# Wide products in the output phase of a recurrent-memory transformer kernel, and left output sums moved to an earlier phase

## The chip, the cores and the metric

The kernel runs on one core of a Trainium2 chip. The metric is the time of one execution in device microseconds. Engines named below: TensorE (PE; its weight loads are PEld), VectorE (DVE), ScalarE (ACT), GpSimd (POOL) and SyncE (SP). SP issues the large transfers, POOL the small ones, ACT those of some intermediate results.

## The reference

The input `x` has 2048 rows of 1024 values. It is normalized by rows (`xn`). Three parts are added: `x` itself, a recurrent attention part A, and a part B that adds a routed feed-forward result to two rows.

Part A is what fills the time. The rows are cut into 64 segments of 32 rows, and 8 rows of memory stand before each:

```python
for s in range(n_seg):
    h = jnp.concatenate([mem, xs], axis=1)          # 8 + 32 rows
    q, k, v = h @ Wq, h @ Wk, h @ Wv                # 32 heads of 128
    p = softmax(mask(q @ k.T * scale))
    o = (p @ v) @ Wo
    mem = o[:, :M, :]                               # the next segment's memory
    outs.append(o[:, M:, :])
```

The memory of one segment is the output of the one before, so the 64 segments follow each other strictly. The four weight matrices are 8 MB each in bf16. Part B picks two rows by a router, and runs them through a gated feed-forward layer at the end.

## The kernel before

**Granules.** The weights are cut into 64 granules of 128 x 2048 values (512 KB): 0 to 47 for q, k and v in the six phases q0, k0, q1, k1, v0, v1 of eight granules each (`PHASES`), and 48 to 63 for the output matrix, two heads each. 44 granules stay in SBUF (`wres`). The 20 of `STREAMED` are read again in every segment from a DRAM copy (`wsc`) into five slots (`g`, `fetch`, L366). A slot's next transfer is issued by SP when PE has released the slot. Granule 6 and half of granule 25 are kept in PSUM instead and copied back by ScalarE and VectorE (`bring_back`, L389; `kept_piece`, L393).

**A segment.** For each granule of a phase four products of 512 columns (L817) add into one PSUM bank, one for each group of 32 columns of the array. PSUM tiles of the tag `acc` have two buffers, used in turn. At the end of a phase ScalarE copies the bank out (XB at L836, VM at L846); PE transposes it (L649), and copies make QT and KT. Scores (L672, L674) and softmax run beside the later phases, `attend` (L736 to L747) beside v1 and the output phase. In the output phase each granule w = 0 to 15 has eight products (`project`, L586): two heads, each 256 columns for each of the four column groups, so that row group g of the bank holds output columns 256 g to 256 g + 255. Then VectorE adds the bank to X, which holds the residual (L885). The result OB is stored by POOL (L887), and its memory rows are transposed (L301) and copied into ST (L324), the left operand of the next segment. Only then can the next segment begin.

**Left rows.** A segment's 32 rows of input are split: 24 go with the 8 rows of memory through the products above. The q, k and v of the other 8 rows don't depend on the memory. Those of four segments (a group, j = 0 to 3) are gathered into 32 rows ahead of time, and their attention outputs likewise behind the group; both take their products through the weights in *passes*: one more set of four products for a granule (`left_pass`, L579, for q, k, v; `project_left`, L598, for the output). The table `PASSES` names for each unit (q0, ..., o) the place (j, phase, granule in the phase) of each pass; phases 7 and 8 stand for the end of a segment, before and after the memory is transposed. These passes fill PE there while VectorE makes L885 and the copy to ST. `COPIES` names the place and the engine that takes a finished unit out of PSUM (`copy_unit`, L627). For q and k units the copy XBl is then stored to DRAM by ACT (`ql_d<-XBl`, L628); a copy by VectorE has its store put off until ScalarE has made VM. The output unit is finished in the first segment of the next group: in `sum_left` the residual OL is prepared by VectorE (L347), two ScalarE copies (L616), two VectorE adds (L619) and one GpSimd add (L620) bring the two halves together, and POOL stores them.

**Order.** The order of every engine's work is that of the program text; `hook(p, kc, fn)` puts `fn` behind granule kc of phase p. Tiles of the pool `one` have one buffer for each tag, and a new tile of a tag waits until all accesses of the last one have ended, transfers included. Three tags (`bx`, `vl0`, `vl1`) change roles from group to group (`roles`); `roles[0]` holds BK, BX or XL, and XBl in turn.

Of the kernel before, what the change touches and what calls it, by code (L numbers as in the profile page):

```python
# [9 lines left out]
F32 = mybir.dt.float32  # L10
# [7 lines left out]
N_RES = 44  # L18
N_SLOT = 5
KEPT_WHOLE = 6  # L20
KEPT_PART = 25
# [22 lines left out]
}  # L44

COPIES = {"q0": (1, 1, 0, "scalar"), "q1": (1, 5, 7, "vector"), "k0": (2, 2, 0, "scalar"), "k1": (2, 5, 7, "vector"),
          "v0": (3, 4, 7, "scalar"), "v1": (3, 5, 7, "scalar"), "o": (0, 3, 3, "vector")}


@with_exitstack  # L50
def kernel(
# [17 lines left out]
    P = 128  # L69
# [203 lines left out]
    def two_rows(m, tag):  # L273
# [3 lines left out]
        return t  # L277

    def load_seg(s):
        for g in range(4):  # L280
            nc.gpsimd.dma_start(out=X[s % 2][32 * g:32 * g + XM, :],  # L281
                                in_=x2[s * SEG:s * SEG + XM, 256 * g:256 * (g + 1)])

# [42 lines left out]
    def load_left(G, t, crossed=False):  # L326

        o4 = x2[4 * G * SEG:4 * (G + 1) * SEG, :].rearrange("(s r) d -> s r d", s=4)[:, XM:SEG, :]
        if not crossed:
            o4 = o4.rearrange("s r d -> r s d")  # L330
        for g in range(4):
            b = 2 * (g % 2) + g // 2 if crossed else g
            nc.gpsimd.dma_start(out=t[32 * g:32 * (g + 1), :], in_=o4[:, :, 256 * b:256 * (b + 1)])
        return t
# [103 lines left out]
    for g in range(4):  # L438
        nc.gpsimd.dma_start(out=OB[32 * g + XM:32 * g + SEG, :], in_=A_mem0[0, :, 256 * g:256 * (g + 1)])
    n_x = 1  # L440
# [140 lines left out]

    def project(PS, w, Gv, lhs, last, first=False):
        for hs in range(2):
            h = 2 * w + hs
            for g in range(4):
                nc.tensor.matmul(PS[32 * g:32 * g + 32, 0:256], lhsT=lhs(h),  # L586
                                 rhs=Gv[:, D * hs + 256 * g:D * hs + 256 * (g + 1)], start=(first and hs == 0),
                                 stop=(last and hs == 1), tile_position=(0, 32 * g), skip_group_check=True)

# [11 lines left out]
    def copy_unit(u, s, engine):  # L601
# [10 lines left out]
        elif u == "o":  # L612
            OL = xl_of[0]
            LF = one.tile([P, 256], F32, tag="otl", name="LF")
            for c in range(2):
                nc.scalar.copy(out=LF[64 * c:64 * c + 64, :], in_=PS[64 - 64 * c:128 - 64 * c, 256 * c:256 * c + 256])  # L616
            for c in range(2):
                here = slice(64 * c, 64 * c + 64)
                nc.vector.tensor_tensor(out=LF[here, :], in0=PS[here, 256 * c:256 * c + 256], in1=LF[here, :], op=ALU.add)  # L619
            nc.gpsimd.tensor_tensor(out=OL[:, :], in0=LF[:, :], in1=OL[:, :], op=ALU.add)  # L620
            o4 = out2[4 * Gu * SEG:4 * (Gu + 1) * SEG, :].rearrange("(s r) d -> s r d", s=4)
            for g in range(4):
                b = 2 * (g % 2) + g // 2
                nc.gpsimd.dma_start(out=o4[:, XM:SEG, 256 * b:256 * (b + 1)], in_=OL[32 * g:32 * (g + 1), :])
# [7 lines left out]
    for s in range(NSEG):  # L632
# [176 lines left out]
        for p, (mat, half) in enumerate(PHASES):  # L809
# [3 lines left out]
            for kc in range(KC):  # L813
                g = 8 * p + kc
                Gv = back if s > 0 and g == KEPT_WHOLE else granule(g)
                for jq in range(4):
                    nc.tensor.matmul(PSm[32 * jq:32 * jq + 32, :], lhsT=ST[:, kc, :], rhs=part(Gv, jq),  # L817
                                     start=(kc == 0), stop=(kc == KC - 1), tile_position=(0, 32 * jq))
# [45 lines left out]
        for w in range(16):  # L864
# [19 lines left out]
        OB = X[s % 2]  # L884
        nc.vector.tensor_tensor(out=OB[:, :], in0=WO[:, 0:256], in1=OB[:, :], op=ALU.add)  # L885
        for g in range(4):
            nc.gpsimd.dma_start(out=out2[s * SEG:s * SEG + XM, 256 * g:256 * (g + 1)], in_=OB[32 * g:32 * g + XM, :])  # L887
        run_passes(7, 0)
# [125 lines left out]
```

## Time and profile before

| | |
|---|---|
| median of 3 runs | 1865.73 us (1863.98 to 1869.82) |
| profiled execution | 1871.21 us, span 1869.1 us |
| mean granted clock | 0.957 |
| PE, PEld busy | 84%, 45% |
| DVE, ACT, POOL busy | 48%, 37%, 24% |
| DMA | 712.27 MB, mean 381 GB/s |

Times are from the span's start. A row of the timeline has start, length, engine, line, operation, what is written and read, the shape and the number of instructions; in brackets is the idle time of the engine before, and what ended it. A row of a table of stretches has the stretch, its length, the busy time of PE, PEld, DVE, ACT and POOL with the number of instructions, the granted clock, the DMA share and GB/s. A row of waits has who waited for whom, the total, the number and the longest.

### The profile page before, as it was taken

To read this page: it belongs to the slowest core of one execution; us is meant where nothing else is said; L and a number is where in the kernel's file an instruction comes from. 1 tells how busy PE (TensorE), PEld (TensorE's weight loads), DVE (VectorE), ACT (ScalarE), POOL (GpSimd) and SP (SyncE) were. 2 spreads that over 40 slices of the span, in tenths; PEclk is the share of its full clock that TensorE was granted. 3 is DMA by queue.
4 is the path that set the end of the run, shared out by engine and by line. 5 is a ranking of instruction groups with operands and counts; after the bars stand their busy time and mean duration, and the time that the engine had idled before them with its cause. 6 is when DMAs were issued, how large, how long until landed. Compare 5 with 4: busy or idle time off the path is not lost.

```text
span 1869.1 us, 80529 instructions
## 1 busy us (share of the span) xinstructions
PE 1568.8 (84%) x34978; PEld 847.9 (45%) x34978; DVE 896.9 (48%) x2950; ACT 683.6 (37%) x1933; POOL 457.1 (24%) x898
## 2 busy tenths in 40 slices
PE   3458998898998988888899988988889988988764
PEld 1124444444444444444444444444445544444433
DVE  6725544554455444544554455544544455445430
ACT  1113433444343433434344334434334343433320
POOL 3111322213231322223132322323132221312220
PEclk8669999999999999999999999999999999999995
DMA  9999999999999999999999999999999999999998
GB/s 370 406 355 373 388 386 380 393 382 387 394 385 392 366 383 391 359 380 385 388 375 388 389 384 387 373 396 374 378 369 396 394 382 383 378 377 352 384 402 338
DMA packets 230322, 712.27 MB, mean 381 GB/s; under 512 B 39040, under 2 KB 52912, under 8 KB 229968
## 3 DMA queue, kind: packets, MB, share of 16 engines
q1 hardware_dynamic: 192592, 671.18, 93.0%
q0 software_dynamic: 28736, 28.08, 4.7%
q10 hardware_dynamic: 8640, 7.87, 1.2%
q8 instruction: 274, 4.49, 0.9%
q14 instruction: 80, 0.66, 0.1%
HBM read 694.32 MB, written 22.29 MB: 383 GB/s over the span
## 4 chain that ended last, share of the span: by engine, by line
DMA 61%; PE 32%; DVE 4%; issue 1%; ACT 1%; SPq 0%; ACTq 0%; DVEq 0%
DMA g<-wsc 54%; PE PSm L817 17%; PE WO L586 4%; PE PSl L579 4%; PE BT L649 2%; DMA XP<-in_A_x_dram 2%; PE WL L598 1%; DMA MW<-in_B_w_gate_dram 1%; DVE XR L256 1%; DMA MW<-in_B_w_up_dram 1%; DMA g<-in_A_Wq_dram 1%; DMA wres<-in_A_Wo_dram 1%; DMA g<-in_A_Wo_dram 1%; DMA MW<-in_B_w_down_dram 1%; DMA g<-in_B_w_down_dram 1%
## 5 line engine op out<-in xcount | busy, mean ns | idle before, releaser
L817 PE MATMUL PSm<-wres,ST 128*32 128x512 bf16 x8448 | 700.5, 383 | 6.5 <-DMA wres<-in_A_Wv_dram 3.5
L817 PEld LDWEIGHTS <-ST 128*32 128x32 bf16 x12288 | 323.6, 96 | 412.7 <-issue 168.2
L817 PE MATMUL PSm<-g,ST 128*32 128x512 bf16 x3588 | 360.0, 386 | 97.7 <-DMA g<-wsc 76.3
L586 PEld LDWEIGHTS <-OT 128*32 128x32 bf16 x8192 | 217.6, 97 | 166.6 <-issue 141.0
L836 ACT CAST XB<-PSm 128x512 bf16<-128x512 f32 x256 | 150.7, 589 | 283.9 <-PE PSm L817 280.8
L586 PE MATMUL WO<-wres,OT 128*32 128x256 bf16 x5632 | 237.6, 278 | 12.3 <-DMA wres<-in_A_Wo_dram 8.0
L495 POOL DMA_DIRECT2D LX<-ql_d x63 | 35.4, 562 | 814.0 <-PE WO L586 423.2
L586 PE MATMUL WO<-g,OT 128*32 128x256 bf16 x2560 | 133.3, 281 | 84.1 <-DMA g<-wsc 72.6
L579 PE MATMUL PSl<-wres,STL 128*32 128x512 bf16 x2112 | 184.5, 390 | 0.4 <-issue 0.4
L887 POOL DMA_DIRECT2D out_dram<-X x256 | 130.2, 515 | 211.9 <-DVE X L885 169.4
L664 DVE COPY KT<-BT 128x512 bf16<-128x512 bf16 x112 | 45.9, 410 | 278.7 <-issue 121.8
L281 POOL DMA_DIRECT2D X<-in_A_x_dram x256 | 130.1, 515 | 179.6 <-PE PSm L817 88.8
L389 ACT COPY BK<-KEPT 128x512 bf16<-128x512 bf16 x126 | 74.3, 590 | 131.2 <-PE WO L586 99.8
L657 ACT COPY QT<-BT 128x512 bf16<-128x512 bf16 x128 | 75.0, 586 | 127.1 <-PE BT L502 78.1
L649 PEld LDWEIGHTS <-XB 128*128 128x128 bf16 x1024 | 58.6, 98 | 117.1 <-ACT XB L836 75.2
L885 DVE TENSOR_TENSOR X<-WO,X 128x256 bf16<-128x256 f32 x64 | 27.2, 425 | 172.3 <-PE WO L586 172.3
L649 PE MATMUL BT<-IDENT,XB 128*128 128x128 bf16 x1024 | 102.2, 223 | 8.2 <-ACT XB L836 6.7
L579 PEld LDWEIGHTS <-STL 128*32 128x32 bf16 x3072 | 84.0, 98 | 53.0 <-issue 8.5
L846 ACT CAST VM<-PSm 128x512 bf16<-128x512 f32 x128 | 76.5, 598 | 83.3 <-PE PSm L817 82.8
L736 PEld LDWEIGHTS <-VM 32*128 32x128 bf16 x2048 | 65.1, 91 | 83.7 <-issue 72.7
L393 DVE COPY g<-KEPT 128x512 bf16<-128x512 bf16 x126 | 47.6, 420 | 101.7 <-PE PSm L817 51.5
L681 DVE TENSOR_TENSOR BS<-BS,CT 128x96 f32<-128x96 f32 (+1 forms) x256 | 59.1, 231 | 72.8 <-PE BS L674 68.3
(175 smaller groups left out, 2371.9 us busy)
## 6 DMA issues: line engine op xcount, KB each, us to landing
g<-wsc SPq DMA_DIRECT2D x1134, 512.0 KB, 6.0
g<-wsc SPq DMA_DIRECT2D x63, 256.0 KB, 5.7
LX<-ql_d POOLq DMA_DIRECT2D x63, 128.0 KB, 5.6
ql_d<-XBl ACTq DMA_DIRECT2D x60, 128.0 KB, 5.8
MW<-in_B_w_gate_dram SPq DMA_DIRECT2D x16, 448.0 KB, 9.5
MW<-in_B_w_up_dram SPq DMA_DIRECT2D x16, 448.0 KB, 9.1
wres<-in_A_Wk_dram SPq DMA_DIRECT2D x12, 512.0 KB, 11.9
MW<-in_B_w_down_dram SPq DMA_DIRECT2D x12, 512.0 KB, 10.1
```

The costliest lines, as they stand in the source:

```text
L281: nc.gpsimd.dma_start(out=X[s % 2][32 * g:32 * g + XM, :], in_=x2[s * SEG:s * SEG + XM, 256 * g:256 * (g + 1)])
L389: copy(out=back[c][:, :], in_=KEPT_COLS[KEPT_WHOLE][c])
L579: nc.tensor.matmul(PSl[32 * jq:32 * jq + 32, :], lhsT=STL[:, g % KC, :], rhs=part(Gv, jq), start=first_, stop=last_, tile_position=(0, 32 ...
L586: nc.tensor.matmul(PS[32 * g:32 * g + 32, 0:256], lhsT=lhs(h), rhs=Gv[:, D * hs + 256 * g:D * hs + 256 * (g + 1)], start=(first and hs == ...
L649: nc.tensor.transpose(out=PTq[:, il, :, :].rearrange("p j r -> p (j r)"), in_=XB[:, il * P:(il + 1) * P], identity=IDENT[:, :])
L657: nc.scalar.copy(out=QT[half][:, :, :], in_=pv)
L681: nc.vector.tensor_tensor(out=S4, in0=S4, in1=m, op=ALU.add)
L736: nc.tensor.matmul(o, lhsT=VM[half][q0:q0 + 32, il * P:(il + 1) * P], rhs=PTm[q0:q0 + 32, il, 0:NK], start=True, stop=False, tile_position ...
L817: nc.tensor.matmul(PSm[32 * jq:32 * jq + 32, :], lhsT=ST[:, kc, :], rhs=part(Gv, jq), start=(kc == 0), stop=(kc == KC - 1), tile_position= ...
L836: nc.scalar.copy(out=XB[:, :], in_=PSm[:, :])
L846: nc.scalar.copy(out=VM[half][:, :], in_=PSm[:, :])
L887: nc.gpsimd.dma_start(out=out2[s * SEG:s * SEG + XM, 256 * g:256 * (g + 1)], in_=OB[32 * g:32 * g + XM, :])
```

## The change

For the first twelve granules of the output phase `project` makes four products of 512 columns in place of eight of 256: the even head goes to row groups 0 and 1, the odd head to 2 and 3, each with both halves of the columns. The two heads' halves then have to be added across partitions (`add_halves`, four VectorE adds of 64 x 256 each): the first two take the bank's halves crosswise and add X, the other two add the straight halves. The result is an f32 tile SUM with the tag `roles[0]`. The last four granules keep the eight products, in a second PSUM tile, and the last add takes SUM in place of X. Since the halves fall into another order, blocks 1 and 2 of 256 columns change places (`block`) in X, in the memory and in the output's stores.

The output unit's last six passes and its copy move ahead in the first segment of a group: the last pass from phase 3 to phase 1, the copy to the end of phase 1, `sum_left` to its middle. The kept pieces of granule 25 are copied one phase earlier. `copy_unit` for the output unit uses `add_halves`: two ScalarE copies, two VectorE adds and the GpSimd add become four VectorE adds. The q0 passes of segment 0's end are made there, no longer in segment 1.

```diff
-          (3, 8, 0): [52, 54], (0, 0, 7): [55], (0, 1, 3): [57], (0, 1, 7): [58], (0, 2, 3): [60], (0, 2, 6): [61],
-          (0, 3, 2): [63]},
+          (3, 8, 0): [52, 54], (0, 0, 3): [55], (0, 0, 7): [57], (0, 1, 2): [58], (0, 1, 4): [60], (0, 1, 5): [61],
+          (0, 1, 6): [63]},
-          "v0": (3, 4, 7, "scalar"), "v1": (3, 5, 7, "scalar"), "o": (0, 3, 3, "vector")}
+          "v0": (3, 4, 7, "scalar"), "v1": (3, 5, 7, "scalar"), "o": (0, 1, 7, "vector")}
+    def block(g):
+        return 2 * (g % 2) + g // 2
-                if s == 0:
+                if s == 0 and at[0] < 7:
                     after_first.append((u, g))
+    def project(PS, w, Gv, lhs):
         for hs in range(2):
             h = 2 * w + hs
+            if w < N_WIDE:
+                for c in range(2):
+                    r0 = 64 * hs + 32 * c
+                    nc.tensor.matmul(PS[r0:r0 + 32, :], lhsT=lhs(h), rhs=Gv[:, D * hs + 512 * c:D * hs + 512 * (c + 1)],
+                                     start=(w == 0), stop=(w == N_WIDE - 1), tile_position=(0, r0), skip_group_check=True)
+                continue
             for g in range(4):
...
+    def add_halves(PS, src, mid, dst):
+        for out, a, flip in ((mid, src, True), (dst, mid, False)):
+            for c in range(2):
+                here = slice(64 * c, 64 * c + 64)
+                there = slice(64 - 64 * c, 128 - 64 * c) if flip else here
+                nc.vector.tensor_tensor(out=out[here, :], in0=PS[there, 256 * c:256 * c + 256], in1=a[here, :], op=ALU.add)
...
-            for c in range(2):
-                nc.scalar.copy(out=LF[64 * c:64 * c + 64, :], in_=PS[64 - 64 * c:128 - 64 * c, 256 * c:256 * c + 256])
-            for c in range(2):
-                here = slice(64 * c, 64 * c + 64)
-                nc.vector.tensor_tensor(out=LF[here, :], in0=PS[here, 256 * c:256 * c + 256], in1=LF[here, :], op=ALU.add)
-            nc.gpsimd.tensor_tensor(out=OL[:, :], in0=LF[:, :], in1=OL[:, :], op=ALU.add)
+            add_halves(PS, OL, LF, OL)
...
-            hook(2, 3, lambda: sum_left(xl_of[0], G - 1))
+            hook(1, 3, lambda: sum_left(xl_of[0], G - 1))
...
-            hook(2, 1, lambda: kept_piece(KEPT_PART, 2, nc.vector.tensor_copy))
-            hook(2, 2, lambda: kept_piece(KEPT_PART, 3, nc.vector.tensor_copy))
+            hook(1, 1, lambda: kept_piece(KEPT_PART, 2, nc.vector.tensor_copy))
+            hook(1, 2, lambda: kept_piece(KEPT_PART, 3, nc.vector.tensor_copy))
...
-            project(WO, w, Gv, lhs_main, w == 15, first=(w == 0))
+            if w == N_WIDE:
+                SUM = one.tile([P, 256], F32, tag=roles[0], name="SUM")
+                add_halves(WO, X[s % 2], SUM, SUM)
+                WO = psA.tile([P, 512], F32, tag="acc", name="WO")
+            project(WO, w, Gv, lhs_main)
...
-        nc.vector.tensor_tensor(out=OB[:, :], in0=WO[:, 0:256], in1=OB[:, :], op=ALU.add)
+        nc.vector.tensor_tensor(out=OB[:, :], in0=WO[:, 0:256], in1=SUM[:, :], op=ALU.add)
```

More of the change, by code (lines that the diff above doesn't have):

```diff
@@ L19 @@
 N_SLOT = 5
+N_WIDE = 12
 KEPT_WHOLE = 6
@@ L331, in load_left @@
         for g in range(4):
-            b = 2 * (g % 2) + g // 2 if crossed else g
+            b = block(g) if crossed else g
             nc.gpsimd.dma_start(out=t[32 * g:32 * (g + 1), :], in_=o4[:, :, 256 * b:256 * (b + 1)])
@@ L438 @@
     for g in range(4):
-        nc.gpsimd.dma_start(out=OB[32 * g + XM:32 * g + SEG, :], in_=A_mem0[0, :, 256 * g:256 * (g + 1)])
+        nc.gpsimd.dma_start(out=OB[32 * g + XM:32 * g + SEG, :], in_=A_mem0[0, :, 256 * block(g):256 * (block(g) + 1)])
     n_x = 1
@@ L816 @@
                 for jq in range(4):
-                    nc.tensor.matmul(PSm[32 * jq:32 * jq + 32, :], lhsT=ST[:, kc, :], rhs=part(Gv, jq),
+                    nc.tensor.matmul(PSm[32 * jq:32 * jq + 32, :], lhsT=ST[:, 2 * block(kc // 2) + kc % 2, :], rhs=part(Gv, jq),
                                      start=(kc == 0), stop=(kc == KC - 1), tile_position=(0, 32 * jq))
@@ L884 @@
         OB = X[s % 2]
-        nc.vector.tensor_tensor(out=OB[:, :], in0=WO[:, 0:256], in1=OB[:, :], op=ALU.add)
+        nc.vector.tensor_tensor(out=OB[:, :], in0=WO[:, 0:256], in1=SUM[:, :], op=ALU.add)
         for g in range(4):
-            nc.gpsimd.dma_start(out=out2[s * SEG:s * SEG + XM, 256 * g:256 * (g + 1)], in_=OB[32 * g:32 * g + XM, :])
+            nc.gpsimd.dma_start(out=out2[s * SEG:s * SEG + XM, 256 * block(g):256 * (block(g) + 1)], in_=OB[32 * g:32 * g + XM, :])
         run_passes(7, 0)
```

10 lines of the change are left out of this document (5 added, 5 removed).

## The prediction

> **What bounds the kernel now.** I read the page first (share by engine, transfers, chain), then the table of stretches for two segments, then the order of time around one segment's end. A segment is one pass of the loop over 32 rows; there are 64.
>
> ```profile
> span 1869.1 us, 80529 instructions
> PE 1568.8 (84%) x34978; PEld 847.9 (45%) x34978; DVE 896.9 (48%) x2950; ACT 683.6 (37%) x1933; POOL 457.1 (24%) x898
> DMA  9999999999999999999999999999999999999998
> q8 instruction: 274, 4.49, 0.9%
> DMA 61%; PE 32%; DVE 4%; issue 1%; ACT 1%; SPq 0%; ACTq 0%; DVEq 0%
> PE BT L301 <- DVE X L885: 2.1, 4, 0.5
> PE PSm L817 <- DMA g<-wsc: 76.3, 154, 2.5
> PE WO L586 <- DMA g<-wsc: 72.6, 150, 2.0
> ```
>
> The DMA engines are 90% busy or more in nearly every slice, and the chain that ended last is 61% DMA. TensorE stands for streamed weights 149 us in all (the last two rows). So weight transfers set most of the pace. VectorE and ScalarE are half idle. But the pace differs by stage:
>
> ```profile
> 1011.04:1016.36 5.32, 4.99 (x88) 2.44 (x88) 1.02 (x3) 1.66 (x3) 1.79 (x5) 1.00 1.02 395
> 1016.36:1021.71 5.35, 5.22 (x117) 2.47 (x113) 2.14 (x6) 2.87 (x6) 2.01 (x4) 1.00 0.94 319
> 1028.52:1036.24 7.72, 5.33 (x170) 4.03 (x170) 3.50 (x15) 2.22 (x9) 0.55 (x1) 1.00 1.02 409
> PE WO L586 <- DMA g<-wsc: 2.4, 3, 1.3
> ```
>
> This is segment 34 (the third of a group of four): the first two phases, the next two, and the output phase. After the length stands PE's busy time; the last number is GB/s. In the first and third stretch data move at 395 and 409 GB/s and PE stands still 0.33 and 2.39 us. In the second PE is busy 5.22 of 5.35 us and the rate is only 319: there the five slots of streamed weights come free at PE's pace. PE time taken out of the output phase is therefore worth nothing by itself; a delay of PE ahead of the second stretch can pass through.
>
> **The wide products.** Twelve of sixteen output granules go from 8 products of 256 columns to 4 of 512. TensorE, at the end of segment 33 and the start of 34:
>
> ```profile
> 1007.73 0.40 PE L586 MATMUL WO<-g,OT 128*32 128x256 bf16 x8 [0.44 <-DMA g<-wsc]
> 1007.95 0.62 PE L586 MATMUL WO<-wres,OT 128*32 128x256 bf16 x16
> 1009.18 0.40 PE L586 MATMUL WO<-g,OT 128*32 128x256 bf16 x8 [0.61 <-DMA g<-wsc]
> 1009.40 0.40 PE L586 MATMUL WO<-wres,OT 128*32 128x256 bf16 x8
> 1009.62 0.83 PE L579 MATMUL PSl<-wres,STL 128*32 128x512 bf16 x12
> 1010.38 0.28 PE L301 MATMUL BT<-IDENT,X 128*128 128x128 bf16 x2
> 1010.60 0.61 PE L579 MATMUL PSl<-wres,STL 128*32 128x512 bf16 x8
> 1011.04 0.60 PE L817 MATMUL PSm<-wres,ST 128*32 128x512 bf16 x8
> 1011.48 0.39 PE L817 MATMUL PSm<-g,ST 128*32 128x512 bf16 x4
> ```
>
> One granule in the old form takes 1009.40 - 1009.18 = 0.22 us from start to start. Two in the four-product form (the form to come) take 1011.48 - 1011.04 = 0.44, again 0.22 each. The four column groups work side by side, so halving the number of products saves next to nothing of PE's pace. What is saved is fetched code: 4.49 MB of code over 2 x 34978 PE instructions is 64 bytes each; 12 x 8 x 64 = 6144 fewer are 0.39 MB, 24 of 274 packets, or 24/274 of 0.9% of the span: 1.5 us of a busy resource. I take -1.5.
>
> **The adds of the halves, and the store they wait for.** The halves of the twelve granules lie in other partitions, so ahead of the last add (L885) VectorE now makes four adds of 64x256, into a new tile SUM. VectorE and the store of the same stretch:
>
> ```profile
> L619 DVE TENSOR_TENSOR LF<-WL,LF x32: 409/422/428, 224.6 to 1812.2; 64x256 f32<-64x256 f32 x32
> 970.18 0.86 DVE L619 TENSOR_TENSOR LF<-WL,LF 64x256 f32<-64x256 f32 x2 [1.05 <-PE PSm L817]
> 1002.72 0.65 DVE L627 CAST XBl<-PSl 128x512 bf16<-128x512 f32 x1
> 1003.40 0.33 ACTq L628 DMA_DIRECT2D ql_d<-XBl  x1
> 1006.86 0.41 DVE L389 COPY BK<-KEPT 128x512 bf16<-128x512 bf16 x1
> 1009.85 0.42 DVE L885 TENSOR_TENSOR X<-WO,X 128x256 bf16<-128x256 f32 x1 [2.57 <-PE WO L586]
> L628 ACTq DMA_DIRECT2D ql_d<-XBl x60: 325/327/361, 136.9 to 1669.2; - x60
> DMA to landing us min/median/max: 4.2/5.8/7.4
> DVE BK L389: 0.3, 1
> 981.91 0.40 PE L586 MATMUL WO<-g,OT 128*32 128x256 bf16 x8 [0.24 <-DMA g<-wsc]
> 983.80 0.42 DVE L885 TENSOR_TENSOR X<-WO,X 128x256 bf16<-128x256 f32 x1 [2.15 <-PE WO L586]
> ```
>
> Two such adds took 0.86 us, so four take 1.72, or +110 us of VectorE work over 64 segments, in which it was idle: 2.57 us before L885. They can start when the twelfth granule's products end, at 1007.73 + 0.40 = 1008.13; L885 follows at about 1008.2 + 1.72 + 0.04 = 1009.96, against 1009.85 now. By itself that is 0.1 us late. In segment 32 (last two rows) the same sum gives 982.31 + 0.05 + 1.76 = 984.1 against 983.80, 0.3 late.
>
> But SUM is given the buffer roles[0]. In the second and third segment of each group this buffer held XBl, copied at 1002.72 (L627), whose store to DRAM is issued only at 1003.40, behind ScalarE's copy of VM. SUM may not be written before that store has read it out and landed: 5.8 us in the median, so 1009.2. (The row on BK shows this dependence in the kernel of before: the buffer's next user waited for the store once, 0.3 us, because it comes later.) Then the adds run from 1009.2 to 1010.95 and L885 starts at 1011.0, 1.1 us later than now. Nothing on VectorE's queue behind the adds is urgent but L885 itself; behind L885 wait the two transposes (PE, 1010.38), the copy to ST, and all of the next segment. PE's filler (12 products from 1009.62) is used up by 1010.4, so PE stands 1.1 us. Sixty stores, two for each segment that has them, one of the two late: 30 segments, 33 us gross.
>
> What hides it: in segment 34 the first two phases have 0.33 us of PE's waits for data, which vanish first; about 0.75 us reaches the second stretch, where the slots are freed at PE's pace. From there to the output phase the loss is real if the late fetches push all later ones, and nothing if the transfers make it up, from 319 GB/s up to 400 (a fifth of 5.35 us, 1.1 us of room). Bounds: 0 and 1.1 us a segment. The second stretch speaks for a loss, the DMA busy in all slices for none; between the two I take half, 0.5 x 30 = +15 us. For the other 34 segments 0.1 to 0.3 us meet about as much waiting: 0 to 10, taken +1.
>
> [...]
>
> **Left output sums earlier, VectorE alone.** In the first segment of a group six left products (0.22 us each) move forward: net one more in phase 0, two more in phase 1, two fewer in phase 2, one fewer in phase 3. Two ScalarE copies, two VectorE adds and GpSimd's add go; four VectorE adds come at the end of phase 1. Segment 32:
>
> ```profile
> 957.77:964.28 6.51, 4.95 (x88) 2.49 (x88) 1.02 (x3) 1.52 (x3) 4.68 (x11) 1.00 1.03 385
> 964.28:969.52 5.24, 5.24 (x120) 2.72 (x116) 2.90 (x11) 2.22 (x6) 1.47 (x3) 1.00 0.93 336
> 964.30 0.60 ACT L836 CAST XB<-PSm 128x512 bf16<-128x512 f32 x1
> 965.96 0.42 DVE L664 COPY KT<-BT 128x512 bf16<-128x512 bf16 x1 [5.91 <-issue]
> 969.40 0.74 ACT L616 COPY LF<-WL 64x256 f32<-64x256 f32 x2
> PE BT L649 <- ACT XB L836: 6.7, 12, 0.6
> PE BS L672 <- DVE BX L715: 2.9, 13, 0.2
> ```
>
> Phases 0 and 1 have 1.56 us of idle PE, so the three products moved there (0.65) are free; phases 2 and 3 are full, so 0.65 us of PE leave a bound stretch. Against it the four adds end 1.72 us after phase 1's last left product (about 963.9 + 1.72 = 965.6) and the KT copy, which would then be wanted at some 965.4, waits up to 0.3 us. The copies at 969.40 delayed the exponent and with it the next XB copy: those waits were 6.7 + 2.9 = 9.6 us in the whole run and should go. Together per group 0.65 - 0.3 + 9.6/15 = 1 us of PE; bounds for 15 groups 0 and -15. Transfers run at 336 to 385 GB/s there, so a third counts: -5 us. The kept pieces move a phase earlier on VectorE with it idle on both sides, 0; GpSimd's output stores go ahead of the next segment's row loads, whose first reader is the output phase, 0; permuted blocks change no size, 0. In segment 0 five left passes fill its end, at most 5 x 0.22 = 1.1 us once.
>
> **Sum.** -1.5 + 15 + 1 - 5 = +9.5, rounded +10 us. The profiled span is 1869.1 us and its execution 1871.2, 5.5 above the median 1865.7 of the runs shown; so a like execution would take 1881, and the median 1876.
>
> **Rivals.**
> *Absorbed.* The transfers make up what PE loses: the store's wait is in the trace but the output phase's 2.39 us of PE waits shrink by as much, and the relief in the first segments is hidden likewise. For it: DMA busy in all slices, 409 GB/s as the highest stretch. Against: 319 GB/s where PE is full. Time 1865, or 1864 with the code fetches. The store landing early (its minimum of 4.2 us puts it at 1007.6, before 1008.13) gives the same.
> *Faster.* The full relief in the first segments of groups, decided by whether PE's stalls behind XB and the full phases 2 and 3 set the pace there: -15, with -1.5 of code, and the store's wait absorbed: about 1853 if all counts, 1858 for half. For: 336 GB/s in a stretch with PE at 5.24 of 5.24. Against: it is one segment in four. It decides from the point where less than a third of the 33 us (11) passes through beside the full relief.
> *Passed through whole.* 33 us, and 3 for the others, with no relief: 1866 + 36 = 1902. For: the second stretch; against: PE's 0.33 us ahead of it and the long waits behind.
> *The change does nothing for PE.* This is part of every case: 0.22 us a granule in both forms.
>
> **How the numbers follow.** Forecast (half passes, 1872 to 1890) 0.43; absorbed 0.25; faster 0.22; passed through 0.10. A measurement of this kernel tells about 0.3%, 5.6 us, from no change (the three runs shown are 5.8 apart). Slower: 0.43 + 0.10 less a little for small sums = 0.52; same 0.26; faster 0.22. The range takes in half of the relief and most of the loss: 1856 to 1896.
>
> **What would show it.** Right: in second and third segments the first of the four adds starts about 1 us after the twelfth granule's end and is released by the store (ql_d<-XBl); L885 moves from 1.7 to about 2.8 us after that end; PE's wait ahead of the transposes on X (2.1 us in all now, in PE's rows) grows to some 30. The output phase's waits for weights shrink by less than that. In first segments the waits of PE on XB (6.7) go. PE's pace stays at 0.22 us a granule. Wrong: if the adds start right behind the twelfth granule, if PE's waits for weights shrink by as much as the new wait adds, or if the granted clock moves.

## The result, and the profile after

The change made the kernel slower: 1919.45 us in the median (1917.74 to 1923.54, six runs) against 1866.83 for the kernel before on the same chip. The ratio is 1.0293, 95% interval 1.0262 to 1.0323, so 53 us are lost by the medians (55 by the ratio) where 10 were forecast. Two executions in the experiments below were far longer than the others of their kernel, one of `busy_out` (2083.93 us, at a granted clock of 0.737) and one of `wide12_x` (2837.26 us), and are left out of every time and ratio given. Lines have moved: the four adds are L606, the last add L902, the wide products L592, the narrow ones L596, the q, k and v products L830, the transposes of X L305, the store of XBl L641.

The page of the changed kernel (span, share by engine, code transfers, all transfers, chain by engine and by line):

```profile
span 1916.1 us, 74850 instructions
PE 1573.6 (82%) x31906; PEld 767.8 (40%) x31906; DVE 1022.5 (53%) x3238; ACT 674.9 (35%) x1901; POOL 443.4 (23%) x882
DMA packets 230303, 711.91 MB, mean 372 GB/s; under 512 B 39040, under 2 KB 52912, under 8 KB 229968
q8 instruction: 250, 4.10, 0.8%
DMA 48%; PE 36%; DVE 12%; issue 2%; ACT 1%; SPq 0%; POOL 0%; DVEq 0%; POOLq 0%; ACTq 0%
DMA g<-wsc 34%; PE PSm L830 22%; DMA ql_d<-XBl 9%; PE PSl L583 5%; DVE SUM L606 4%; PE BT L662 3%; PE WO L592 2%; PE WL L616 1%; DMA MW<-in_B_w_gate_dram 1%; DVE X L902 1%; DVE XR L257 1%; DMA g<-in_A_Wq_dram 1%; DMA MW<-in_B_w_up_dram 1%; PE BT L305 1%; DVE XBl L640 1%
```

Code went from 274 packets to 250, as worked out, and VectorE from 897 to 1022 us (the adds ahead of the last one had been put at 110, those of the output unit come on top). TensorE has 3072 products fewer (31906 for 34978) and is no less busy (1574 for 1569 us). New is the chain: 9% of it is the store `ql_d<-XBl`, 12% VectorE; before, VectorE had 4%.

The waits of the changed kernel (who waited for whom, total, number, longest):

```profile
DVE SUM L606 <- DMA ql_d<-XBl: 67.0, 26, 4.6
PE BT L305 <- DVE X L902: 54.3, 51, 3.3
PE PSm L830 <- DMA g<-wsc: 85.9, 160, 2.1
PE WO L592 <- DMA g<-wsc: 45.8, 95, 1.6
PE WO L596 <- DMA g<-wsc: 29.2, 56, 1.6
```

TensorE's wait for X grew from 2.1 to 54.3 us. Its waits for streamed weights should have shrunk in exchange if the transfers caught up; they are 161 us (the last three rows) against 149 before. So nothing was made up over the run: 54.3 - 2.1 = 52 us is as much as the whole loss.

One such segment end, in the order of time (the second segment of a group, number 33). It is among the longest: TensorE stands 2.63 us here, and 1.48 us in the mean of the 30 second and third segments that have such a store.

```profile
1030.90 0.33 ACTq L641 DMA_DIRECT2D ql_d<-XBl  x1
1034.57 0.40 PE L592 MATMUL WO<-g,OT 128*32 128x512 bf16 x4 [0.84 <-DMA g<-wsc]
1036.29 0.83 PE L583 MATMUL PSl<-wres,STL 128*32 128x512 bf16 x12
1037.38 0.88 DVE L606 TENSOR_TENSOR SUM<-WO,X 64x256 f32<-64x256 f32 x2 [3.65 <-DMA ql_d<-XBl]
1038.28 0.88 DVE L606 TENSOR_TENSOR SUM<-WO,SUM 64x256 f32<-64x256 f32 x2
1039.26 0.43 DVE L902 TENSOR_TENSOR X<-WO,SUM 128x256 bf16<-128x256 f32 x1
1039.75 0.39 PE L305 MATMUL BT<-IDENT,X 128*128 128x128 bf16 x2 [2.63 <-DVE X L902]
```

The twelfth granule ends at 1034.97. The store was issued at 1030.90; the view of its line in this stretch gives the time to its landing:

```profile
DMA to landing us min/median/max: 6.4/6.4/6.4
```

So it lands at 1037.3, and only then do the adds begin, 2.4 us after the products they need. From the first of them to the start of the last add it is 1.88 us, and TensorE, whose filling of twelve left products ended at 1037.12, stands 2.63 us. What the transfers do around it stands in the table of stretches, first after and then before (the last three numbers of a row are the granted clock, the DMA share and GB/s):

```profile
1037.50:1039.50 2.00, 0.00 (x0) 0.00 (x0) 1.80 (x5) 0.00 (x0) 0.00 (x0) 1.00 1.05 424
1039.50:1041.00 1.50, 1.25 (x14) 0.50 (x18) 0.72 (x3) 0.00 (x0) 1.02 (x3) 0.50 0.98 391
1041.00:1043.50 2.50, 2.50 (x36) 0.98 (x32) 0.07 (x1) 0.00 (x0) 1.22 (x3) 0.62 0.24 82
1043.50:1047.00 3.50, 3.50 (x68) 1.74 (x64) 0.68 (x2) 1.98 (x4) 2.01 (x4) 1.00 0.71 244
```

```profile
1010.40:1012.00 1.60, 1.60 (x34) 0.76 (x31) 0.53 (x2) 0.08 (x1) 1.43 (x3) 1.00 0.98 394
1012.00:1014.50 2.50, 2.17 (x40) 0.81 (x32) 0.76 (x2) 0.59 (x1) 0.83 (x3) 1.00 1.03 415
1014.50:1018.00 3.50, 3.37 (x60) 1.69 (x59) 0.00 (x0) 2.15 (x4) 0.73 (x2) 1.00 0.98 349
```

During the stand the transfers go on at 424 GB/s. Then no slot is free: SyncE, which issues them, waits for TensorE to release one, as its row from 1036 to 1046 says.

```profile
SPq L370 <- PE PSm L830: 5.4, 2, 4.8
```

From 1041.0 the DMA engines move 82 GB/s at a share of 0.24. At about the same place before they moved 415. So the stand is lost for the transfers too. The segment shown is an extreme, but not alone. From 1.25 to 3.75 us behind the start of the transposes the rate is 282 GB/s in the mean of the 30 segments, against 398 before; four of the 30 lie below 100, and none did before. (The table shows a second thing, a granted clock of 0.50 behind the stand; the last experiments are about it.)

### The profile page after: what moved, and what is told of

It is laid out like the page before. It is cut to its first block, busy times and chain, and to the rows that moved or that the text cites. A ratio compares the mean times of both kernels' runs of the same rounds, so it can differ in the third digit from the quotient of the medians.

```text
span 1916.1 us, 74850 instructions
## 1 busy us (share of the span) xinstructions
PE 1573.6 (82%) x31906; PEld 767.8 (40%) x31906; DVE 1022.5 (53%) x3238; ACT 674.9 (35%) x1901; POOL 443.4 (23%) x882
## 4 chain that ended last, share of the span: by engine, by line
DMA 48%; PE 36%; DVE 12%; issue 2%; ACT 1%; SPq 0%; POOL 0%; DVEq 0%; POOLq 0%; ACTq 0%
DMA g<-wsc 34%; PE PSm L830 22%; DMA ql_d<-XBl 9%; PE PSl L583 5%; DVE SUM L606 4%; PE BT L662 3%; PE WO L592 2%; PE WL L616 1%; DMA MW<-in_B_w_gate_dram 1%; DVE X L902 1%; DVE XR L257 1%; DMA g<-in_A_Wq_dram 1%; DMA MW<-in_B_w_up_dram 1%; PE BT L305 1%; DVE XBl L640 1%
## 5 line engine op out<-in xcount | busy, mean ns | idle before, releaser
L830 PE MATMUL PSm<-wres,ST 128*32 128x512 bf16 x8448 | 709.8, 388 | 6.7 <-DMA wres<-in_A_Wv_dram 4.1
L830 PEld LDWEIGHTS <-ST 128*32 128x32 bf16 x12288 | 328.1, 97 | 427.0 <-issue 178.8
L830 PE MATMUL PSm<-g,ST 128*32 128x512 bf16 x3588 | 363.3, 391 | 107.0 <-DMA g<-wsc 85.9
L592 PE MATMUL WO<-wres,OT 128*32 128x512 bf16 x2048 | 168.2, 395 | 8.7 <-DMA wres<-in_A_Wo_dram 8.5
L592 PE MATMUL WO<-g,OT 128*32 128x512 bf16 x1024 | 105.4, 399 | 54.8 <-DMA g<-wsc 45.8
L592 PEld LDWEIGHTS <-OT 128*32 128x32 bf16 x3072 | 85.8, 97 | 157.6 <-issue 108.1
L606 DVE TENSOR_TENSOR SUM<-WO,X 64x256 f32<-64x256 f32 x128 | 54.1, 422 | 108.3 <-DMA ql_d<-XBl 67.0
L758 DVE CAST OT<-BT 128x128 bf16<-128x128 f32 x128 | 37.3, 291 | 124.5 <-PE BT L305 65.1
```

Of the source, the lines that this page charges most:

```text
L592: nc.tensor.matmul(PS[r0:r0 + 32, :], lhsT=lhs(h), rhs=Gv[:, D * hs + 512 * c:D * hs + 512 * (c + 1)], start=(w == 0), stop=(w == N_WIDE - ...
L606: nc.vector.tensor_tensor(out=out[here, :], in0=PS[there, 256 * c:256 * c + 256], in1=a[here, :], op=ALU.add)
L830: nc.tensor.matmul(PSm[32 * jq:32 * jq + 32, :], lhsT=ST[:, 2 * block(kc // 2) + kc % 2, :], rhs=part(Gv, jq), start=(kc == 0), stop=(kc = ...
```

## The experiments

Kernels are compared with the kernel before, run beside them; in brackets is the 95% interval of the ratio. A loss in us is the ratio less one, times the median of before in that comparison (1867 to 1870 us). The kernels named `..._x` or `six_wide9...` keep the sums of halves in X, rounded to bf16. Of the longer edits the main lines are printed. The added products of zeros, the copies of a bank onto itself and the claimed buffer change no output.

**Which part costs what.** In `sum_in_x` the changed kernel makes its sum in X, so nothing waits for the store:

```diff
-                SUM = one.tile([P, 256], F32, tag=roles[0], name="SUM")
-                add_halves(WO, X[s % 2], SUM, SUM)
+                SUM = X[s % 2]
+                add_halves(WO, SUM, SUM, SUM)
```

> The changed kernel with SUM kept in X (bf16) in place of the buffer roles[0]: the same four adds, no store to wait for; the half sums are rounded to bf16 once more. Theory A (the last add is late because the adds queue behind the store, and PE's stand at a segment's end passes through whole): PE's waits for X after a store go from 1.67 and 1.32 us to 0.2, the rest of 0.1 to 0.4 us a segment stays; 8 to 14 us over before, some 40 us below the changed kernel. Rival (the cause lies in the wide products or in the moved sums): still over 30 us above before.

Measured: 1876.04 us, ratio 1.0032 (1.0003 to 1.0062). TensorE's wait for X falls to a fifth:

```profile
PE BT L305 <- DVE X L902: 11.7, 25, 1.5
```

The same four adds (0.42 us each in both), the same moved passes, the same wide products, without the store ahead of them: 2.6 of the 2.9% are gone, and the 0.3% left are as much as the moves cost alone (below). The 6 us over before are a little less than theory A's 8 to 14, and far from the rival's 30.

`wait_alone` does the opposite. It takes the kernel before and lets VectorE claim the buffer of roles[0] behind the twelfth granule, with one column set to zero, and adds nothing else:

```diff
+            if w == 12:
+                SUM = one.tile([P, 256], F32, tag=roles[0], name="SUM")
+                nc.vector.memset(SUM[:, 0:1], 0.0)
```

> The kernel before, with a new tile claimed in roles[0] by VectorE (one column set to zero) at the twelfth granule, nothing else: the store's wait without the adds. Theory A: the store lands 1.0 to 1.3 us after the twelfth granule's end, the last add comes 1.7 us after it, so the wait is hidden in most segments: 0 to 4 us over before. Rival (the wait itself, by blocking VectorE, is the price): 15 us or more.

Measured: 1871.57 us, 1.0025 (0.999 to 1.0059). In its waits VectorE stands for the store as foreseen, and TensorE hardly for X:

```profile
DVE SUM L875 <- DMA ql_d<-XBl: 39.3, 20, 3.1
PE BT L301 <- DVE X L888: 3.4, 7, 0.5
```

So the wait by itself costs nothing that can be told, and hardly makes TensorE wait for X; and the adds by themselves (`sum_in_x`) cost little. Only in a row, the adds behind the wait, do they reach past the sixteenth granule and the left products behind it.

`moves_only` takes the moved passes, the output unit's sum by VectorE and the kept pieces into the kernel before, with its eight narrow products:

```diff
-          (3, 8, 0): [52, 54], (0, 0, 7): [55], (0, 1, 3): [57], (0, 1, 7): [58], (0, 2, 3): [60], (0, 2, 6): [61],
-          (0, 3, 2): [63]},
+          (3, 8, 0): [52, 54], (0, 0, 3): [55], (0, 0, 7): [57], (0, 1, 2): [58], (0, 1, 4): [60], (0, 1, 5): [61],
+          (0, 1, 6): [63]},
...
-            hook(2, 3, lambda: sum_left(xl_of[0], G - 1))
+            hook(1, 3, lambda: sum_left(xl_of[0], G - 1))
```

> The kernel before with the left output passes, their sums by VectorE and the kept pieces moved as in the change; products and last add as before. Theory A: PE's waits for XB in first segments go (9 us in all), the transfers set the pace: -5 to +1 us against before. Rival (bunching the passes in the k phase costs): 10 us or more over before.

Measured: 1874.32 us, 1.0036 (1.0001 to 1.0071). TensorE's waits behind XB and BX, 6.7 and 2.9 us before, no longer appear among its waits, but those for weights are 159 us instead of 149. The loss of 7 us lies between the two theories.

```profile
PE PSm L819 <- DMA g<-wsc: 94.4, 186, 2.1
PE WO L586 <- DMA g<-wsc: 64.8, 133, 1.8
```

`wide_only` is the changed kernel with these moves taken back.

> The changed kernel without the moves: wide products, four adds, SUM in roles[0], left sums where they were. Theory A: all of the loss is here, 45 to 55 us over before. Rival (the moves make part of the loss): 30 us or less over before.

Measured: 1911.35 us, 1.0212 (1.0153 to 1.0271).

```profile
PE BT L305 <- DVE X L907: 50.3, 48, 2.9
```

The 40 us (29 to 51) lie between theory A (45 to 55) and its rival (30 or less) and decide for neither. 2.1% and 0.4% make 2.5%, against 2.9% for both; the intervals overlap, so no extra cost of the two together is shown.

**How much of a late segment end passes.** `late1` and `late3` put one or three VectorE copies of the bank onto itself ahead of the last add of the kernel before:

```diff
         OB = X[s % 2]
+        for _ in range(1 if s + 1 < NSEG else 0):        # late3: 3
+            nc.vector.tensor_copy(out=WO[:, 0:256], in_=WO[:, 0:256])
         nc.vector.tensor_tensor(out=OB[:, :], in0=WO[:, 0:256], in1=OB[:, :], op=ALU.add)
```

> The kernel before with the last add of each segment made late by one VectorE operation (WO copied onto itself, about 0.46 us), without any wait for a store. PE should stand 0.4 us at each end, 25 us in all. Theory A (whatever PE stands at a segment's end passes through whole): 20 to 28 us over before. Theory T (a short stand is made up by transfers already queued, only what is longer passes): 0 to 10 us.

> The same with three such operations, 1.38 us late: PE stands 1.3 us at each end, 82 us in all. Theory A: 75 to 90 us over before. Theory T: 40 to 65 us. Theory B of the prediction (transfers make up half): about 41 us.

Measured: 1880.52 us, 1.0046 (1.0018 to 1.0073), and 1927.4 us, 1.0319 (1.0267 to 1.037). The rows of `late1` and then of `late3`:

```profile
PE BT L301 <- DVE X L887: 23.1, 57, 1.0
```

```profile
PE BT L301 <- DVE X L887: 79.9, 61, 1.9
PE WO L586 <- DMA g<-wsc: 73.5, 149, 1.7
PE PSm L817 <- DMA g<-wsc: 61.9, 124, 1.6
```

Of 21 us of new stand (23.1 - 2.1) some 9 passed; of 78 some 60, and the waits for weights gave back 14 (149 to 135). Theory T had both. Two kernels add the low end: `wide12_x` and `wide9_x` take the wide products for twelve and for nine granules into the kernel before, with the sum in X and without the moves.

```diff
+N_WIDE = 12        # wide9_x: 9
...
+            if w == N_WIDE:
+                SUM = X[s % 2]
+                add_halves(WO, SUM, SUM, SUM)
+                WO = psA.tile([P, 512], F32, tag="acc", name="WO")
```

> The same with twelve granules: the last add is late by 0.2 to 0.5 us, PE stands 0.1 to 0.35 us at an end, 11 us in all. Theory T (short stands are made up): -4 to +4 us against before. Theory A: +8 to +12. The changed kernel in X with the moves was 6 over before, the moves alone 7 over, so -1 if they add up.

> The kernel before with wide products for nine granules, the four adds kept in X (half sums rounded to bf16 once more), nothing moved: the adds end about 1 us before the last products. Theory A: nothing is late, PE's pace is the same, 5 to 6% less code: -5 to +1 us against before. If the wide products themselves cost something (banks, adds beside products): 5 us or more over.

Measured: `wide12_x` 1867.89 us, 0.9991 (0.9957 to 1.0024), and `wide9_x` 1865.95 us, 0.997 (0.9941 to 0.9998). `wide12_x` has this wait for X:

```profile
PE BT L305 <- DVE X L907: 10.8, 30, 1.0
```

`wide9_x`, where the adds begin three granules earlier, has none of note. So the wide products with a harmless sum are worth nothing that can be told in the one form, and 0.3% at best in the other, with an interval that ends just below no change. It is the only kernel of all whose interval lies below 1, and among some twenty intervals one may do so by chance.

New stand against loss, by the rows and ratios above:

| kernel | new wait for X, us | loss, us |
|---|---|---|
| wide12_x | 9 | -2 |
| sum_in_x | 10 | 6, no more than the moves alone (7) |
| late1 | 21 | 9 |
| wide_only | 48 | 40 |
| after | 52 | 55, the moves (7) among it |
| late3 | 78 | 60 |

Each loss is known to 5 to 11 us (half of its interval). In the four rows without the moves 8 to 18 us of the stand don't show up in the time; of the two large stands among them (`wide_only`, `late3`) some four fifths do.

**TensorE time in other places.** `busy_q1` adds 24 products of zeros with 512 columns in the third phase, `busy_wide` the same number behind the second output granule, `busy_out` 48 with 256 columns there. By TensorE's pace (0.22 us for four of 512 columns or eight of 256) each is an estimated 1.3 us a segment, 84 us in all. `ZERO` is a tile of zeros; the lines of the three kernels stand below one another.

```diff
+                if g == 16:                                              # busy_q1
+                    for n in range(24):
+                        nc.tensor.matmul(PSm[32 * (n % 4):32 * (n % 4) + 32, :], lhsT=ZERO[:, :], rhs=part(Gv, n % 4),
+                                         start=False, stop=False, tile_position=(0, 32 * (n % 4)))
...
+            if w == 1:                                                   # busy_out
+                for _ in range(6):
+                    project(WO, w, Gv, lambda h: ZERO[:, :], False)
...
+            for n in range(24 if w == 1 else 0):                         # busy_wide
+                nc.tensor.matmul(WO[32 * (n % 4):32 * (n % 4) + 32, :], lhsT=ZERO[:, :], rhs=Gv[:, 512 * (n % 4):512 * (n % 4 + 1)],
+                                 start=False, stop=False, tile_position=(0, 32 * (n % 4)), skip_group_check=True)
```

> The kernel before with 24 products of zeros (512 columns, 1.3 us of PE) added behind the first granule of phase 2, where PE is full and transfers run at 320 to 350 GB/s. If the slots follow PE there, as the prediction had it, nearly all passes: 65 to 85 us over before. If the transfers make it up in the value and output phases: under 40 us.

> The kernel before with 48 products of zeros (256 columns, 1.3 us of PE) added behind the second granule of each output phase, where PE waits 1.4 to 1.8 us for weights later in the phase in three segments of four. Theories A and T alike for this place: PE's waits for weights shrink by what is added, 15 to 30 us over before (the fourth segment of a group has no such waits). If PE time is lost wherever it is taken: 80 us.

> The zeros of the output phase (1.3 us of PE) as 24 products of 512 columns in place of 48 of 256, so half the code for the same time; the 48 were 76 to 81 us over before with waits on PE of 45 us that no row explains. If those are late code: 25 to 55 us over before, with few such waits. If PE time is lost there anyway: 70 us or more.

Measured: `busy_q1` 1949.5 us, 1.0426 (1.0371 to 1.0481); `busy_out` 1946.34 us (two executions), 1.041 (1.0337 to 1.0484); `busy_wide` 1918.67 us, 1.028 (1.023 to 1.033). In the third phase 80 of 84 us pass. In the output phase 52 do in `busy_wide`; `busy_out`, with twice as many products for the same time, seemed to say 77, but in its waits a row has grown that was 5.5 us before, and it is less than half as large in `busy_wide`. The rows of `busy_out`, then of `busy_wide`:

```profile
PE WO L588 <- issue: 45.3, 45, 2.4
```

```profile
PE PSm L819 <- DMA g<-wsc: 87.3, 180, 2.7
PE WO L588 <- DMA g<-wsc: 25.0, 47, 1.5
PE WO L588 <- issue: 19.8, 26, 1.8
```

"issue" is time in which TensorE waited for nothing that the profile shows. That code arrived late for the dense small products would fit, and is not shown. The output phase does hold room (its waits for weights fell from 72.6 to 25.0 us, while those of the other phases rose from 76.3 to 87.3), but more than half of the added time passes even there.

`late3_mid` puts the three copies behind the second output granule instead.

```diff
+            for _ in range(3 if w == 1 else 0):
+                nc.vector.tensor_copy(out=WO[:, 0:256], in_=WO[:, 0:256])
```

> The kernel before with the three in-place copies of WO (1.4 us, PE has to wait for them) behind the second granule of each output phase instead of the segment's end, with no more code on PE: 88 us of standing in all. Theory S (a stand is made up only where PE waits for weights afterwards in the same phase; the end of a segment has none): 15 to 45 us over before. If PE's stands are lost wherever they are: 75 us or more, as at the segment's end.

Measured: 2022.33 us, 1.0851 (1.078 to 1.0922). As a test of the place it failed: the stand is 2.5 us a segment and not the 1.3 of `late3`, and the mean granted clock fell to 0.913, with TensorE busy for 1615 us instead of 1569. All the same it is no sign of room: of 161 us of stand as many as 159 are lost, though the waits for weights of the output phase are no longer among TensorE's rows.

```profile
PE WO L586 <- DVE WO L876: 161.3, 64, 3.6
PE PSm L817 <- DMA g<-wsc: 105.4, 181, 2.2
```

**Is it the depth of the slots?** `six_slots` gives the weights a sixth slot; one more granule is streamed in exchange.

```diff
...
-N_RES = 44
-N_SLOT = 5
+N_RES = 43
+N_SLOT = 6
-STREAMED = [2, 5, 6, 9, 13, 17, 21, 25, 29, 33, 36, 39, 42, 45, 47, 50, 53, 56, 59, 62]
+STREAMED = [2, 5, 6, 9, 13, 17, 21, 25, 29, 33, 36, 39, 42, 45, 47, 50, 53, 56, 58, 59, 62]
...
```

`six_late3` adds the copies of `late3` to it, `six_wide9` the products of `wide9_x`.

> The kernel before with six slots in place of five; for the room granule 58 is streamed as well (21 granules a segment, its left pass made as it streams), so 5% more bytes. No theory parts here: 1900 to 1960 us, as the base for the next run.

> The same with the last add made late by three operations (PE stands 1.28 us at each end, which cost the kernel with five slots 58 to 60 us, about 0.95 us of each 1.28). Theory S (a stand passes because the transfers run out of free slots; a sixth slot covers one more transfer, 1.3 us): 0 to 35 us over the kernel with six slots. If slots don't decide (the chain of PE's work sets the segment's length by itself): 50 us or more over it.

> Six slots (43 resident granules) and nine granules in the wide form with the adds kept in X, nothing moved. Both parts alone were 0.0 and -0.3% against before. If PE's chain with its code sets the length where slots are in plenty, they add up: -0.2 to -0.8% against before. If transfers at 400 GB/s set it: 0.0% as with six slots alone, or slower.

Measured: `six_slots` 1867.38 us, 1.0005 (0.9978 to 1.0033); `six_late3` 1918.64 us, 1.0284 (1.0242 to 1.0325); `six_wide9` 1869.75 us, 1.0013 (0.9992 to 1.0034). A line of the page of `six_slots`, its waits, and the waits of `six_late3`:

```profile
DMA packets 239539, 745.83 MB, mean 399 GB/s; under 512 B 40064, under 2 KB 53936, under 8 KB 239184
```

```profile
PE WO L586 <- DMA g<-wsc: 92.6, 150, 2.1
PE PSm L817 <- DMA g<-wsc: 23.2, 57, 1.6
```

```profile
PE BT L301 <- DVE X L887: 79.0, 63, 1.9
PE WO L586 <- DMA g<-wsc: 75.3, 121, 1.3
PE PSm L817 <- DMA g<-wsc: 3.6, 11, 0.8
```

The sixth slot moved 34 MB more in the same time, 399 for 381 GB/s; the expected 1900 to 1960 us were far off. So the DMA engines, "90% or more" busy in nearly every slice before, were not at their limit. With the stand of `late3` the waits for weights gave back more than with five slots, 37 us (116 to 79) in place of 14. From 1.25 to 3.75 us behind the start of the transposes, in the mean of 60 segment ends, the stand lowered the rate only from 395 to 380 GB/s; with five slots it lowered it from 386 to 323. So the lack of a free slot stops the transfers behind a stand, and a sixth slot eases that. Yet the price of the same stand is 53 us (45 to 61) in place of 60 (50 to 69). These overlap, so not even this gain is shown. Most of the stand passes with six slots too. SyncE's rows of `six_slots` name one reason why the slot may give less than it could. Its transfers wait for the store of XBl, for which they waited 0.3 us before:

```profile
SPq L366 <- DMA ql_d<-XBl: 101.6, 58, 3.6
```

Six slots without these waits were not tried. `six_wide9` shows no gain either, so the two parts did not add up to one.

**Is it the clock?** The trace shows a granted clock of 0.50 behind the stand at 1039.5, and the mean clock of the profiled executions fell from 0.957 to 0.949. In `after_warm` the changed kernel gets forty small products of zeros in the stands of the two segments that wait for the store, 1.1 us each:

```diff
+        for n in range(40 if j in (1, 2) else 0):
+            nc.tensor.matmul(WO[32 * (n % 4):32 * (n % 4) + 32, 0:256], lhsT=ZERO[:, :], rhs=res_tiles[63][:, 0:256],
+                             start=False, stop=False, tile_position=(0, 32 * (n % 4)), skip_group_check=True)
         OB = X[s % 2]
```

`six_warm` and `six_wide9_warm` put sixteen behind output granule 10 and eight behind granule 13 of the two kernels with six slots, in three segments of each group, where TensorE waits for weights.

> The changed kernel with forty products of a zero tile by 256 columns (0.11 us a four, 1.1 us in all) put on TensorE behind the sixteenth output granule of the second and third segment of a group: they add zeros to the second output bank and fill a part of the stand in which TensorE waits for X. The adds, the store they wait for and the last add are as in the changed kernel. Theory A (a part of the loss is the clock: the profile of the changed kernel shows the granted clock at half for 3.4 us behind 9 of the long stands, and 22 us of lost clock more than before over the whole run): the granted clock rises from 0.949 to 0.953 to 0.957, TensorE's wait for X shrinks by the filling (54 to some 25 us), and the time falls by 8 to 20 us, to 1900 to 1911. Theory B (the late adds alone are the loss and the clock costs nothing, since the transfers set the pace): the wait for X shrinks likewise, but the time stays at 1916 to 1923, or grows where a stand was shorter than the filling.

> Six slots (43 resident granules, 5% more bytes) with sixteen products of a zero tile behind output granule 10 and eight behind granule 13, in three segments of each group: 0.43 and 0.22 us where TensorE waits for weights for about 1.1 and 0.5 us a segment. Theory A (six slots gave nothing because the deeper lead was paid for by the clock: 0.947 against 0.959): the granted clock rises to 0.952 or more and the time falls from the 1867 of six slots by 4 to 12 us, to 1855 to 1863, below the kernel before. Theory B (transfers set the pace of the output phase whatever the clock does): 1864 to 1870, the clock higher and the waits for weights shorter by the filling.

> The same filling in the kernel with six slots, nine granules of wide products and the sum made in X (rounded to bf16), which ran at 1870 with the lowest clock of all, 0.943. Theory A: the clock rises to 0.95 or more and the time falls to 1855 to 1864. Theory B: 1866 to 1872.

Measured: `after_warm` 1917.95 us, 1.0287 (1.026 to 1.0314); `six_warm` 1905.16 us, 1.0202 (1.0178 to 1.0226); `six_wide9_warm` 1903.15 us, 1.0197 (1.0174 to 1.0219). The clock of `after_warm`, and two of its waits:

```profile
core 0: 1906.2 us, clock 0.957
```

```profile
PE BT L307 <- DVE X L907: 14.7, 36, 1.5
PE PSm L832 <- DMA g<-wsc: 93.4, 173, 1.8
```

The stands are filled (54.3 to 14.7 us), the clock is back at 0.957, and the time is what it was, within some 8 us by the two intervals. (Stands that had been shorter than the filling's 1.1 us became longer by it, an estimated 4 us in all by the stands of `after`.) So the slower clock behind these stands cost little. That this is because the transfers set the pace, as theory B has it, is argued. `six_warm` raised the clock too, from 0.951 in the profile of `six_slots` to 0.958, and lost 38 us (33 to 42), more than the 32 us that its products take by TensorE's pace (0.66 us in 48 segments). Both theories on it missed, and on `six_wide9_warm` too. Its rows:

```profile
PE WO L588 <- DMA g<-wsc: 73.6, 166, 1.6
PE PSm L819 <- DMA g<-wsc: 28.4, 79, 1.3
PE WO L588 <- issue: 22.8, 27, 2.3
```

The waits for weights shrank by 14 (116 to 102) and those that nothing explains grew by 13 (9.4 to 22.8). Here the time in which TensorE waits for weights could not be filled for free. Why the loss is larger than the filling stays open.

## Why the prediction was right or wrong

*The wide products, -1.5: borne out as far as can be told.* A granule takes 0.22 us in the new form too (two starts of `after` at 1031.61 and 1031.83), TensorE's busy time hardly moved with 3072 products fewer, and `wide12_x`, these products with adds that meet no wait, lies at 0.9991. A term of 1.5 us is below what these intervals tell.

*The adds wait for the store: right in mechanism, too small in size.* Who waits, for what and in which segments came out as written; `sum_in_x` and `wait_alone` show that it takes the store and the adds in a row. The term was 1.1 us in 30 segments, 33 us gross. It measured 1.48 us in the mean of the 30, 44 us. Two numbers in it were short. From the issue of the store to the first add it is 6.19 us in the mean, where the median landing of all sixty stores was taken, 5.8. From the first of the four adds to the last add it is 1.89 us, where 1.8 were taken. The end of TensorE's filling was right (7.0 us behind the issue of the store, measured 7.08).

*"Half passes": this is the step that failed.* For the transfers to make up a stand they must run ahead during it or faster behind it. They did run ahead, but they were nearly as far ahead as they can be: in the segment shown SyncE soon waited 4.8 us for a free slot, and in the mean of the 30 segments the rate behind the stand was 282 GB/s where it had been 398. The long waits of the output phase, which the prediction took for room, are not room for this: over the run the waits for weights went from 149 to 161 us (the moves alone raise them to 159). Of new stands of 48 and 78 us some 40 and 60 passed (`wide_only`, `late3`), and not half; only of the short stands of `late1`, 21 us, was it 9. Half of the measured 44 would still have been 22 us. The prediction read the DMA share of 90% in all slices as a resource that is always at work and would catch up; `six_slots` shows that 5% more could be moved in the same time. That full slots stop the transfers behind a stand is shown. That they are all of why the stand passes is not: with a sixth slot the rate hardly falls there, and most of the stand passes all the same. What carries the loss there stays open.

*"Passed through whole" had 0.10.* It was the nearest rival. Its 1902 was short by the size of the stand and by the sign of the relief; that a part of each stand does not show up in the time (the table above) goes the other way.

*The relief in first segments, -5 of PE and transfers: wrong in sign.* The waits on XB and BX went as foreseen. But TensorE's waits for streamed weights rose, 159 us in `moves_only` for 149, and the kernel took 7 us more (0 to 13). A third of the relief had been counted as time won, and none was. The new waits for weights eat up the old ones for XB and BX; what the loss beyond that consists of is not shown.

*Others, +1: borne out as far as can be told.* Outside the 30 segments some 8 us of new stand remain, 0.1 to 0.4 us a segment and near the 0.1 to 0.3 worked out, and in `sum_in_x`, where these adds are late in the same way, they cost nothing that can be told from the moves.

*The granted clock.* The prediction named a moving clock as a sign against it. It moved, by 0.008, as a follower of the stands; `after_warm` shows that it is not where most of the time went.

*The sums.* -1.5, +15, +1 and -5 were forecast. By the experiments they are about 0, +40 for the second and third together (`wide_only`), and +7, in all 47; the 55 of the whole change lies within the intervals of that sum. One sum of the prediction is wrong in itself: the full case of *Faster*, -15 and -1.5 from 1866, gives 1849 and not 1853. Nothing else hangs on it.

## What to carry to other kernels

Before giving a new tile an old buffer, look up when the last access of that buffer ends, transfers included, and what stands behind the new tile in its engine's queue: a wait that is free by itself (`wait_alone`, 1.0025) and work that costs little by itself (`sum_in_x`, 1.0032) can miss a deadline when they stand in a row (the changed kernel, 1.0293). In a kernel with a fixed number of prefetch slots look at the transfer rate right behind a stand of the consumer, not at the mean, and at whom the issuing engine waits for. Here a rate that fell there from 386 to 323 GB/s (`late3`) went with some 60 of 78 us that passed; a rate that nearly held (`six_late3`, 395 to 380) was no proof that the stand does not pass. Waits of 6.7 and 2.9 us taken off an engine that waits for transfers a little later were worth nothing here (`moves_only`, 1.0036).

## What the runs showed of the hardware beyond that

- A DMA share near 1 in every slice is no proof of a full machine: the rate was 381 GB/s with five slots and 399 with six, at a share of 90% or more in nearly every slice of both.
- The granted clock fell to 0.50 behind stands of TensorE: in the stretches shown, behind a stand of 2.63 us, it is 0.50 for 1.5 us and 0.62 on the mean of the next 2.5, which makes 1.5 + 2.5 x 0.38 / 0.5 = 3.4 us at the half. In `after` each of the nine longest stands for X, 1.87 to 3.33 us, was followed by 3.4 us at half the clock (beginning from 0.4 us before the end of the stand to 1.3 us behind it), and none of the next three, 1.58 to 1.80 us. In `late3_mid`, with stands of 2.5 us in each segment, the mean clock was 0.913.
- Behind small products in a dense row TensorE stood for something that the profile does not name: 45.3 us with 48 products a segment (`busy_out`), 19.8 with 24 of twice the columns (`busy_wide`), 5.5 with none (before).
- The 128 KB store of XBl took 4.2 us from issue to landing at the least, 5.8 in the median and 7.4 at the most (sixty of them, before), beside a stream of weights at 381 GB/s.
